# Two operand tiles behind the weights in SBUF, and four reorderings ahead of the first layer

## The chip, the core and the metric

The program runs on one core of one Trainium2 chip. The metric is the device time of one execution in microseconds (us), as a median of runs. A core has five engines that run side by side and wait for one another by semaphores: TensorE (PE, with weight loads listed as PEld), VectorE (DVE), ScalarE (ACT), GpSimd (POOL) and SyncE (SP, which here only issues DMA transfers). SBUF is the on-chip memory of 128 partitions; PSUM holds TensorE's results in eight banks.

## What is computed

```python
kv = np.einsum('bhsd,bhse->bhde', k, v)            # attention without softmax: 8 x 8 heads,
out = np.einsum('bhsd,bhde->bhse', q, kv)          # 576 tokens, 64 wide
out = out / sqrt(mean(out * out) + 1e-6) * g_norm
x = out.transpose(0, 2, 1, 3).reshape(4608, 512)

h = x @ w_in                                       # 512 -> 2048
g = np.maximum(h, 0.0) + alpha * np.minimum(h, 0.0)
x = g @ w_out                                      # 2048 -> 512

e = argmax(x @ w_gate + modality_bias[modality_id])  # one of 8 experts for each token
out[token] = gate * (relu(x @ w1[e]) @ w2[e])        # 512 -> 1024 -> 512
```

Every matrix product of the two dense stages is made of three: each fp32 operand is split in a high part, rounded to the fp32r type, and a low part, the remainder; high times high, high times low and low times high are summed in PSUM.

## The kernel before, in words

**Phase one** goes over the 4608 tokens in nine chunks of 512 (c = 0 to 8). In a chunk, 16 steps go over blocks of 128 of the 2048 hidden columns: `first` (L404) makes a block of h with 12 matmuls of 512 columns, and `second` (L431) adds the block before it to y with 12 more. In L404 the weights W are the stationary operand (128 columns, loaded ahead of each matmul) and x's parts, `xhi` and `xlo`, are the moving one (512 columns). In L431 the parts of g (tile g2, "g" in the rows) are stationary and W moves.

**Phase two** takes blocks of 128 tokens of one expert, 41 in all. Each has 24 matmuls of its first layer and 24 of its second, all recorded at L714. In the first layer `xhi` and `xlo` (which now hold the gathered rows' parts) are stationary and the expert's weights, again in W, move; in the second the parts of the hidden values (`hth`, `htl`) are stationary and W moves.

**SBUF.** The pool `one` lays its tiles out in the order in which the code allocates them, each start rounded up to 32 bytes. In the built program W begins at byte 4,224 of each partition and takes 131,072 bytes. Behind it come `ident`, `alpha_sb`, `less`, `g_sb`, four `yrow`, `tri`, `ones`, `wg_sb`, several small tables, two `kvbd` and `kx`, together 41,952 bytes, and only then `xhi` at byte 177,248 and `xlo` at 185,440 (8,192 bytes each). The tiles g2 and hth lie at 220,992 and 225,088, htl at 206,656, 210,752 or 214,848. So `xhi` and `xlo` start 32 bytes past a multiple of 64, as do the 128- and 512-column pieces that the matmuls read of them; W, g2, hth and htl and their pieces start on multiples of 64.

**PSUM.** Banks 0 to 3 belong to the pool `ps_y` (y, and ahead of phase one `kvp`, `ops` and `first`), banks 4 and 5 to `ps_h` (h), bank 6 to `a`, bank 7 is the tile `spare`. In phase two h takes banks 4 to 7.

**Ahead of the first layer**, the order on every engine is the order in which the code is written; there is no scheduler. For the first chunk, by function and line:

- `kv_pair(p)` (L284, L287): k'v of two heads on TensorE, copied to `kvbd` by VectorE (L289).
- `attend_pair(p)` (L293): the attention of two heads into four PSUM tiles `ops` (`a`, `spare` and two of `ps_y`).
- `square_half(t, h)` (L304, ScalarE) and `sum_half(t, h)` (L309, VectorE): squares and their sums for half the heads of token tile t, h = 0 for pairs 0 and 1, h = 1 for pairs 2 and 3.
- The first block of weights is rebuilt from its raw bits: `cut_a(0)` casts (L165, ScalarE), `low_bits(0)` (L174, VectorE), `high_bits(0)` joins both (L179, GpSimd), `cut_c(0)` writes W's high part (L190, ScalarE) and low part (L191, GpSimd).
- `rsqrt(0)`: `half` on GpSimd (L338), then VectorE's iteration from `u` (L339) to `root` (L345).
- `scale_first(h)` (L369): the scaled x, on VectorE for most tiles, on GpSimd for tile 2 and half of tile 3.
- `turn_first((0, 1))` and `turn_first((2, 3))` (L379): TensorE transposes x into four PSUM tiles, one for each block k of 128 columns.
- `take_x(0, k)`: xhi (L391, ScalarE) and xlo (L392, VectorE); then the loop begins with `first(0, 0)`, which takes its four xlo matmuls as late as it can.

A run of 36 transposes of the identity (`warm`, L885) keeps TensorE occupied while the scaling factors are made.

Of the kernel before, what the change touches and what calls it, by code (L numbers as in the profile page):

```python
# [8 lines left out]
F32 = mybir.dt.float32  # L9
F32R = mybir.dt.float32r  # L10
# [16 lines left out]
CT = 512  # L27
NT = CT // 128
# [22 lines left out]
def fused(ctx: ExitStack, tc, qT, kv, kv0, g2, wmoe, alpha, wgate, bias, modality, w12, out):  # L51
# [8 lines left out]
    one = ctx.enter_context(tc.tile_pool(name="one", bufs=1))  # L60
    two = ctx.enter_context(tc.tile_pool(name="two", bufs=2))
    dram = ctx.enter_context(tc.tile_pool(name="dram", bufs=1, space=DRAM))
    ps_y = ctx.enter_context(tc.tile_pool(name="ps_y", bufs=4, space=PSUM))
# [3 lines left out]
    spare = phase1.enter_context(tc.tile_pool(name="ps_s", bufs=1, space=PSUM)).tile([128, 512], F32, name="spare")  # L67
# [3 lines left out]
    xb = dram.tile([E * BUCKET + 1024, ROW], F32, name="xb")  # L71

    W = one.tile([128, 2 * SLOT], F32R, name="W")
    ident = one.tile([128, 128], F32, name="ident")
    alpha_sb = one.tile([128, NFB], F32, name="alpha_sb")
    less = one.tile([128, NFB], F32, name="less")
# [12 lines left out]
    kx = one.tile([128, 2560], F32, name="kx")  # L89
    xs = [kx[:, t * D:t * D + D] for t in range(NT)]  # L90
    xr = kx[:, 0:3 * D].rearrange("p (t c) -> p t c", c=D)
    xhi = one.tile([128, 4, CT], F32R, name="xhi")
    xlo = one.tile([128, 4, CT], F32R, name="xlo")
    junk = one.tile([128, D], F32, name="junk")
    tail = one.tile([128, NIT, 2], F32, name="tail")
    tab_pe = one.tile([1, 8], I32, name="tab_pe")
# [9 lines left out]
    def bank(n):  # L106
        return ps_h.tile([128, n], F32, tag="h", name="h")
# [28 lines left out]
    def w_at(fb, part):  # L136
        o = fb * 2048 + part * 512
        return W[:, o:o + 512]

# [20 lines left out]
    def cut_a(n):  # L160
        if n >= 2 * NFB:
            return

        a = yrow[(n + 1) % 3 if n else 0][:, 0:512]
        A.copy(a.bitcast(F16).rearrange("p (a b) -> p a b", b=2)[:, :, 1:2], raw_t[n].bitcast(BF16)[:, :, 2:3])  # L165
        cut_t[n] = a
# [111 lines left out]
    def kv_pair(p):  # L278

        t = kv_t.pop((0, p))  # L280
        kvp = ps_y.tile([128, 128], F32, tag="y", name="kvp") if p < 2 else bank(128)
        for k in range(4):
            o = k * 256
            PE.matmul(kvp, t[:, o:o + 128], t[:, o + 128:o + 256], start=(k == 0), stop=False)  # L284
        for o in (0, 64):
            r = slice(o, o + 64)
            PE.matmul(kvp[r, r], t[r, 1024:1088], t[r, 1088:1152], start=False, stop=True)  # L287
        for o in (0, 64):
            V.tensor_copy(kvbd[0][o:o + 64, p, o:o + 64], kvp[o:o + 64, o:o + 64])  # L289

    def attend_pair(p, ts=range(NT)):
        for t in ts:
            PE.matmul(ops[t][:, p, :], q_t[0][:, p, t * 128:(t + 1) * 128], kvbd[0][:, p, :], start=True, stop=True)  # L293
# [3 lines left out]
    def square_half(t, h):  # L297
        if t < 2:
            sq = (junk, yrow[3])[t][:, h * 256:h * 256 + 256]
        else:  # L300
            if not sq4:
                sq4.append(two.tile([128, CT], F32, tag="gg", name="sq", bufs=1))
            sq = sq4[0][:, (t - 2) * 256:(t - 1) * 256]
        A.activation(sq, ops[t][:, 2 * h:2 * h + 2, :].rearrange("p a b -> p (a b)"), AF.Square)  # L304
        sq_t[t, h] = sq

    def sum_half(t, h):
        o = t * 8 + h * 4
        V.tensor_reduce(ms_t[0][:, o:o + 4], sq_t.pop((t, h)).rearrange("p (a b) -> p a b", b=64), AX.X, ALU.add)  # L309
# [63 lines left out]
    first_x = []  # L373

    def turn_first(ks):
        pair = [ps_y.tile([128, CT], F32, tag="y", name="first") if k < 2 else spare if k == 2 else bank(CT) for k in ks]
        for t in range(NT):
            for k, ps in zip(ks, pair):
                PE.transpose(ps[:, t * 128:(t + 1) * 128], xs[t][:, k * 128:(k + 1) * 128], ident)  # L379
        return pair  # L380
# [255 lines left out]
    def load_expert(j, halves=(0, 1)):  # L636
# [4 lines left out]
        for half in halves:  # L641
# [3 lines left out]
            at = (j & 1) * SLOT + o  # L645
            d = SP.dma_start(W[:, at:at + SLOT // 2].bitcast(F32), wsp[ds(eid, 1), :, o:o + SLOT // 2].rearrange("a p c -> p (a c)"))
            tc.add_to_no_dep_group("experts", d.ins)
# [64 lines left out]
    def mm(i, ps, a, o, start, stop, late=False):  # L712
        w = (W if i < EARLY else regs[i][0])[:, o:o + 512]
        m = PE.matmul(ps, a, w, start=start, stop=stop)  # L714
        if i:
            tc.declare_no_dep(m.ins, group="experts", reason="sem_w says that the weights are in")
        if late:
            tc.declare_no_dep(m.ins, group=f"first half {i}", reason="of another bank")
# [3 lines left out]
    def layer1(i, between=None):  # L722
        if i >= EARLY:
# [5 lines left out]
            j, slot = PE.snap(j, min_val=0, max_val=7), PE.snap(slot, min_val=0, max_val=SLOT)  # L729
            regs[i] = W[:, ds(slot, SLOT)], j * 2 + 2  # L730
            PE.wait_ge(sem_w, j * 2 + 1)
# [129 lines left out]
    with tc.manual_schedule():  # L861
# [18 lines left out]
        def warm(n):  # L880
            if n == 0:
                return
            ps = bank(128)
            for _ in range(n):
                PE.transpose(ps, ident, ident)  # L885
# [12 lines left out]
        attend_pair(1)  # L898
        for t in range(NT):
            square_half(t, 0)  # L900
        kv_pair(3)
        for t in range(NT):
            sum_half(t, 0)
        attend_pair(2)
        attend_pair(3)
        for t in range(NT):
            square_half(t, 1)
        cut_a(0)
        warm(WARM[5])
        low_bits(0)  # L910
        high_bits(0)
# [16 lines left out]
        G.tensor_scalar(less, alpha_sb, -1.0, 1.0, ALU.mult, ALU.add)  # L928
        load_q(1)
        first_x.extend(turn_first((0, 1)) + turn_first((2, 3)))  # L930
        for k in range(4):
            take_x(0, k)
# [247 lines left out]
```

## Time and profile before

| | us |
|---|---|
| median of 3 runs | 1339.71 (1338.65 to 1340.37) |
| the profiled execution's own time | 1338.95 |
| its span, first to last instruction | 1337.3 |
| TensorE busy | 1326.1 (99%) |
| VectorE busy | 987.1 (74%) |
| GpSimd busy | 649.0 (49%) |
| ScalarE busy | 521.8 (39%) |

The profiled execution is 0.76 us under the median, and 1.65 us of it lie outside the span. A busy TensorE is not one at its peak: its matmuls overlap in the records (one lasts some 390 ns, while they start some 230 ns apart), so the distance between starts is read, from the timeline.

### The profile page before, as it was taken

The page shows a single profiled execution, that of the slowest core. Times are in us where ns is not written, and L with a number is a line of the kernel's source. Part 1 is how long each engine was busy: PE and PEld are TensorE (multiplying, and loading weights), DVE is VectorE, ACT ScalarE, POOL GpSimd, SP SyncE. Part 2 cuts the span into 40 slices and gives each one's busy share as a digit, 9 for nine tenths or more (in the row PEclk, how much of TensorE's full clock was granted, in tenths as well). Part 3 has the DMA queues.
Part 4 walks back from the last instruction along what each step waited for, and adds up shares of the span by engine and source line. Part 5 has one row for each costly group of instructions (what it writes and reads, how often), then busy time and mean ns, then how long its engine had stood idle before and what let it go on. Part 6 is the DMA issues. An engine that isn't in the chain of part 4 may idle for free.

```text
span 1337.3 us, 24668 instructions
## 1 busy us (share of the span) xinstructions
PE 1326.1 (99%) x8096; PEld 1074.1 (80%) x8096; DVE 987.1 (74%) x2052; ACT 521.8 (39%) x1093; POOL 649.0 (49%) x605
## 2 busy tenths in 40 slices
PE   9999999999999999999999999999999999999997
PEld 7878887888888878888888888788888888888886
DVE  5568977968959869869779779386766666666664
ACT  4665233233232332331332321154544444444443
POOL 4655556566465565565565652363333333333321
PEclk9999999999999999999999999999999999999999
DMA  9656456566376375475463530817411261737784
GB/s 339 226 176 217 162 201 228 176 229 227 126 257 213 107 265 189 143 272 170 161 234 113 190 116 0 306 41 258 177 48 48 84 260 49 283 104 297 295 332 175
DMA packets 81883, 250.56 MB, mean 187 GB/s; under 512 B 12829, under 2 KB 32029, under 8 KB 78560
## 3 DMA queue, kind: packets, MB, share of 16 engines
q1 hardware_dynamic: 70000, 220.82, 46.3%
q0 software_dynamic: 11760, 28.14, 6.5%
q8 instruction: 72, 1.18, 0.4%
q14 instruction: 51, 0.42, 0.1%
HBM read 158.69 MB, written 91.54 MB: 187 GB/s over the span
## 4 chain that ended last, share of the span: by engine, by line
PE 57%; issue 30%; POOL 5%; DVE 4%; DMA 2%; POOLq 2%; SPq 1%; ACT 0%; ACTq 0%; DVEq 0%
PE h L404 27%; PE y L431 26%; DVE junk L448 1%; PE a L240 1%; POOL kx L671 1%; POOL raw L227 1%; POOL g L417 1%; POOL out_dram L822 1%; DMA out_dram<-kvbd,tail 1%; POOLq L667 1%; PE a L265 1%; PE h L714 1%; POOLq L671 1%; PE spare L265 1%; DVE gg L410 0%
## 5 line engine op out<-in xcount | busy, mean ns | idle before, releaser
L431 PE MATMUL y<-W,g 128*128 128x512 f32 x1728 | 419.9, 392 | 0.9 <-ACT g L416 0.9
L404 PE MATMUL h<-xhi,W 128*128 128x512 f32 x1152 | 387.0, 398 | 0.0
L431 PEld LDWEIGHTS y<-W,g 128*128 128x128 f32 x1728 | 324.2, 188 | 74.1 <-ACT g L416 2.7
L417 POOL TENSOR_TENSOR g<-gg,g 128x512 fp32r<-128x512 f32 x144 | 216.8, 1506 | 335.4 <-ACT g L416 306.8
L448 DVE CUSTOM_DVE_ANT_0 junk<-yrow,wg_sb 128x512 f32<-128x512 f32 x256 | 273.9, 1070 | 6.4
L416 ACT CAST g<-gg 128x512 fp32r<-128x512 f32 x144 | 89.5, 621 | 441.2 <-DVE gg L411 387.2
L404 PEld LDWEIGHTS h<-xhi,W 128*128 128x128 f32 x1152 | 216.2, 188 | 52.0 <-issue 0.8
L404 PE MATMUL h<-xlo,W 128*128 128x512 f32 x576 | 225.9, 395 | 0.0
L714 PE MATMUL h<-W,xhi 128*128 (+1 forms) x656 | 206.4, 396 | 0.1
L714 PE MATMUL y<-W,hth 128*128 (+1 forms) x656 | 204.4, 393 | 0.0
L227 POOL TENSOR_TENSOR raw<-raw 128x512 f32<-128x512 f32 x128 | 193.6, 1517 | 14.9 <-ACT raw L223 14.7
L410 DVE TENSOR_SCALAR gg<-h,alpha_sb 128x512 f32<-128x512 f32 x128 | 95.7, 748 | 107.5 <-PE h L404 85.9
L822 POOL DMA_INDIRECT out_dram<-kvbd,tail x41 | 43.4, 1059 | 255.4 <-ACT kvbd L820 220.7
L714 PEld LDWEIGHTS h<-W,xhi 128*128 128x128 f32 x656 | 122.7, 187 | 30.2 <-issue 0.5
L714 PEld LDWEIGHTS y<-W,hth 128*128 128x128 f32 x656 | 123.1, 188 | 26.6
L768 DVE TENSOR_SCALAR hh<-h 32x256 f32<-32x256 f32 (+1 forms) x320 | 129.0, 403 | 7.4 <-PE h L714 2.4
L714 PE MATMUL h<-W,xlo 128*128 (+1 forms) x328 | 129.3, 394 | 0.0
L404 PEld LDWEIGHTS h<-xlo,W 128*128 128x128 f32 x576 | 108.2, 188 | 24.8 <-DVE xlo L392 0.3
L714 PE MATMUL y<-W,htl 128*128 (+1 forms) x328 | 127.6, 389 | 0.0
L768 ACT ACTIVATE hh<-h 32x256 f32<-32x256 f32 (+1 forms) x320 | 117.1, 366 | 23.3 <-PE h L714 17.7
L795 DVE TENSOR_TENSOR htl<-hh,hth 128x512 fp32r<-128x512 f32 x76 | 52.6, 693 | 97.5 <-ACT hth L788 97.4
L223 ACT CAST raw<-raw 128x512 fp32r<-128x512 f32 x128 | 78.5, 618 | 59.4 <-DMA raw<-in_w_dram 47.5
(226 smaller groups left out, 1262.3 us busy)
## 6 DMA issues: line engine op xcount, KB each, us to landing
wsp<-raw SPq DMA_DIRECT2D x128, 512.0 KB
W<-wsp SPq DMA_DIRECT2D x16, 4096.0 KB
raw<-in_w_dram SPq DMA_DIRECT2D x128, 256.0 KB
kx<-in_kv_dram SPq DMA_DIRECT2D x28, 512.0 KB
kx<-xb POOLq DMA_DIRECT2D x140, 64.0 KB
raw<-in_wmoe_dram SPq DMA_DIRECT2D x17, 511.8 KB
qT<-in_qT_dram SPq DMA_DIRECT2D x8, 1024.0 KB
wg_sb<-in_wmoe_dram SPq DMA_DIRECT2D x15, 511.8 KB
```

The costliest lines, as they stand in the source:

```text
L223: A.copy(sp_t[n][:, 0:512].bitcast(F32R), sp_t[n][:, 512:1024])
L227: G.tensor_tensor(lo, lo, hi, ALU.subtract)
L404: PE.matmul(ps, w_at(fb, part)[:, k * 128:(k + 1) * 128], x[:, k, :], start=(i == 0), stop=(i == 11))
L410: V.tensor_scalar(gg, ps, 0.0, alpha_sb[:, fb:fb + 1], ALU.min, ALU.mult)
L416: A.copy(ghi, gg)
L417: G.tensor_tensor(glo, gg, ghi.bitcast(F32), ALU.subtract)
L431: PE.matmul(y_t[c][t], a[:, t * 128:(t + 1) * 128], w, start=(fb == i == 0), stop=(fb == NFB - 1 and i == 2))
L448: V.tensor_tensor_reduce(junk, y, wg_sb[:, e, :], 1.0, 0.0, ALU.mult, ALU.add, lg_t[c][:, t, e:e + 1])
L714: m = PE.matmul(ps, a, w, start=start, stop=stop)
L768: m = V.tensor_scalar(to, of, 0.0, None, ALU.max) if mine else A.activation(to, of, AF.Relu)
L795: V.tensor_tensor(order(lo[:, n]), h[:, n].rearrange("p (a c j) -> p c a j", c=4, a=4), order(hi[:, n]).bitcast(F32), ALU.subtract)
L822: d = G.indirect_dma_start(out=out, out_offset=IndirectOffsetOnAxis(ap=tail[:, i, 1:2].bitcast(I32), axis=0), in_=y, in_offset=None, bound ...
```

## The change

`xhi` and `xlo` are allocated right behind W. In the built program they then start at 135,296 and 143,488, both multiples of 128; the tiles that stood between W and them move up by 16,384 bytes, and those behind them stay where they were. Nothing else of the loops changes: the same matmuls stand in the same order.

Ahead of the first layer, the sums of the first half come before `kv_pair(3)`, the weight's cast `cut_a(0)` before the second squares, and the turned block k = 2 goes to a tile of `ps_y` in the place of `spare`; `turn_first` takes the token tiles in the order 0, 2, 1, 3.

```diff
@@ tiles
     W = one.tile([128, 2 * SLOT], F32R, name="W")
+    xhi = one.tile([128, 4, CT], F32R, name="xhi")
+    xlo = one.tile([128, 4, CT], F32R, name="xlo")
     ident = one.tile([128, 128], F32, name="ident")
...
     xr = kx[:, 0:3 * D].rearrange("p (t c) -> p t c", c=D)
-    xhi = one.tile([128, 4, CT], F32R, name="xhi")
-    xlo = one.tile([128, 4, CT], F32R, name="xlo")
     junk = one.tile([128, D], F32, name="junk")
@@ turn_first
-        pair = [ps_y.tile([128, CT], F32, tag="y", name="first") if k < 2 else spare if k == 2 else bank(CT) for k in ks]
-        for t in range(NT):
+        pair = [ps_y.tile([128, CT], F32, tag="y", name="first") if k < 3 else bank(CT) for k in ks]
+        for t in (0, 2, 1, 3):
@@ ahead of the first layer
             square_half(t, 0)
-        kv_pair(3)
         for t in range(NT):
             sum_half(t, 0)
+        kv_pair(3)
         attend_pair(2)
         attend_pair(3)
+        cut_a(0)
         for t in range(NT):
             square_half(t, 1)
-        cut_a(0)
         warm(WARM[5])
```

On ScalarE, between the first squares and the copies of the attention's result, the program of before has these rows (a number behind a name tells buffers apart; yrow_83 is the weight's buffer):

```order
L304 ACTIVATE sq<-ops 128x256 x2
L304 ACTIVATE junk<-a 128x256
L304 ACTIVATE yrow_86<-spare 128x256
L304 ACTIVATE sq<-ops 128x256 x2
L165 CAST yrow_83<-raw 128x512
L915 COPY yrow_84<-ops 128x512
```

and the changed one these, where the weight's buffer is yrow_85:

```order
L304 ACTIVATE sq<-ops 128x256 x2
L165 CAST yrow_85<-raw 128x512
L304 ACTIVATE junk<-a 128x256
L304 ACTIVATE yrow_88<-spare 128x256
L304 ACTIVATE sq<-ops 128x256 x2
L915 COPY yrow_86<-ops 128x512
```

The cast of the first weight's raw bits has moved ahead of four squares.

On VectorE, from the copies of k'v to the end of the sums, before (kvbd_96 is the first of the two k'v tiles):

```order
L289 COPY kvbd_96<-h 64x64 x4
L309 TENSOR_REDUCE ms<-junk 128x4
L309 TENSOR_REDUCE ms<-yrow_86 128x4
L309 TENSOR_REDUCE ms<-sq 128x4 x2
L174 TENSOR_SCALAR wg_sb<-raw 128x512
```

and changed:

```order
L289 COPY kvbd_98<-h 64x64 x2
L309 TENSOR_REDUCE ms<-junk 128x4
L309 TENSOR_REDUCE ms<-yrow_88 128x4
L309 TENSOR_REDUCE ms<-sq 128x4 x2
L289 COPY kvbd_98<-h 64x64 x2
L174 TENSOR_SCALAR wg_sb<-raw 128x512
```

The four sums have moved ahead of the last two copies.

## Rows read from the trace of the kernel before

**Rows 1.** The page: busy time by engine, and TensorE's granted clock in tenths
```profile
PE 1326.1 (99%) x8096; PEld 1074.1 (80%) x8096; DVE 987.1 (74%) x2052; ACT 521.8 (39%) x1093; POOL 649.0 (49%) x605
...
PEclk9999999999999999999999999999999999999999
```

**Rows 2.** Timeline, TensorE, fifth chunk: start us, us, engine, line, operation, out<-in, count
```profile
399.55 4.74 PE L431 MATMUL y<-W,g 128*128 128x512 f32 x20
404.13 0.40 PE L404 MATMUL h<-xhi,W 128*128 128x512 f32 x1
...
406.93 1.08 PE L431 MATMUL y<-W,g 128*128 128x512 f32 x4
```

**Rows 3.** Timeline, TensorE, the two layers of expert blocks, same columns
```profile
1202.68 0.63 PE L714 MATMUL h<-W,xhi 128*128 x2
...
1208.05 0.39 PE L714 MATMUL h<-W,xlo 128*128 x1
1208.27 0.62 PE L714 MATMUL y<-W,hth 128*128 x2
...
1213.54 0.40 PE L714 MATMUL y<-W,htl 128*128 x1
```

**Rows 4.** The page's groups: line, engine, operation, out<-in, count | busy us, mean ns | idle
```profile
L404 PE MATMUL h<-xhi,W 128*128 128x512 f32 x1152 | 387.0, 398 | 0.0
...
L404 PE MATMUL h<-xlo,W 128*128 128x512 f32 x576 | 225.9, 395 | 0.0
L714 PE MATMUL h<-W,xhi 128*128 (+1 forms) x656 | 206.4, 396 | 0.1
...
L714 PE MATMUL h<-W,xlo 128*128 (+1 forms) x328 | 129.3, 394 | 0.0
```

**Rows 5.** Timeline, TensorE, attention of the first chunk, three PSUM tiles in turn
```profile
10.79 0.39 PE L293 MATMUL a<-kvbd,qT 128*128 128x128 f32 x2
...
11.01 0.39 PE L293 MATMUL spare<-kvbd,qT 128*128 128x128 f32 x2
...
11.23 0.61 PE L293 MATMUL ops<-kvbd,qT 128*128 128x128 f32 x4
```

**Rows 6.** Timeline, start to first layer; in brackets idle time and releaser
```profile
4.75 1.47 PEld L284 LDWEIGHTS kvp<-kx 128*128 128x128 f32 x8 [0.34 <-DMA kx<-in_kv_dram]
...
14.35 0.38 ACT L304 ACTIVATE junk<-a 128x256 f32<-128x256 f32 x1 [1.93 <-PE a L293]
...
15.42 0.80 ACT L165 CAST yrow<-raw 128x512 f16<-128x512 bf16 x1
...
15.84 0.73 DVE L309 TENSOR_REDUCE ms<-sq 128x4 f32<-128x256 f32 x2
...
16.35 1.28 POOL L179 TENSOR_TENSOR yrow<-yrow,wg_sb 128x512 int32<-128x512 int32 x1 [7.34 <-DVE ms L309]
...
17.97 0.19 DVE L339 TENSOR_TENSOR u<-h,half 128x32 f32<-128x32 f32 x1 [0.94 <-POOL half L338]
...
18.37 1.27 POOL L191 TENSOR_TENSOR W<-yrow,W 128x512 fp32r<-128x512 f32 x1 [0.43 <-ACT W L190]
...
20.31 1.21 PE L379 MATMUL first<-ident,kx 128*128 128x128 f32 x8 [1.40 <-DVE kx L369]
...
21.73 0.30 PE L379 MATMUL spare<-ident,kx 128*128 128x128 f32 x1 [0.21 <-DVE kx L369]
...
22.55 1.18 PE L404 MATMUL h<-xhi,W 128*128 128x512 f32 x4
...
24.15 0.74 DVE L392 SCALAR_TENSOR_TENSOR xlo<-h,g_sb,xhi 128x512 fp32r<-128x512 f32 x1
```

**Rows 7.** Windows: stretch, length, busy time by engine, clock, DMA share, GB/s
```profile
0.00:4.15 4.15, 2.58 (x12) 2.59 (x13) 0.97 (x2) 1.28 (x1) 3.19 (x25) 1.00 0.50 172
0.00:12.00 12.00, 10.38 (x73) 9.44 (x74) 2.30 (x8) 2.07 (x4) 3.75 (x26) 1.00 0.83 297
12.00:14.00 2.00, 2.00 (x20) 1.81 (x19) 0.91 (x4) 0.42 (x2) 0.00 (x0) 1.00 1.02 420
```

## The prediction, made before the changed kernel ran

> **What bounds the kernel now.** I read the page's shares first. [...] So nearly every microsecond is either a matmul's turn on TensorE or the start, and the question is how far apart matmuls start. That I read from starts in the timeline, not from the mean durations of some 390 ns, which overlap.
>
> In phase one, 20 matmuls of L431 go from 399.55 to 404.13, 4.58 us or 229.0 ns each, and then 12 of L404 from 404.13 to 406.93, 2.80 us or 233.3 ns each [rows 2]. In phase two the 24 of the first layer have 23 spacings from 1202.68 to 1208.05, 5.37 us or 233.5 ns each, and the 24 of the second 23 from 1208.27 to 1213.54, 5.27 us or 229.1 ns [rows 3]. All have 128 stationary and 512 moving columns of the same type, none waits, and yet there are two classes, 4.3 to 4.4 ns apart. The start has its own chain: TensorE waits 1.40 us for scaled x ahead of its first transposes, and VectorE 0.94 us for GpSimd ahead of that [rows 6].
>
> **The tiles' place.** What have the two slow classes in common? Not the shape, and not the role: xhi and xlo move in L404 and are stationary in phase two's first layer. W is in the quick classes as well. Two things are left: the slow ones alone read xhi and xlo, the only large operands here that start 32 bytes past a multiple of 64, and they write PSUM banks 4 to 7, the quick ones 0 to 3. Against the banks stands the first chunk's attention, which goes from bank 6 to bank 7 to two banks of the first four: groups start at 10.79, 11.01 and 11.23, two matmuls in 0.22 us in bank 6 as in bank 7, and the four of the last group take no longer each [rows 5] (these are 128-column matmuls, so they don't settle it). Distance from W doesn't fit either: the tiles at 206,656 and beyond are quick, those at 177,248 are slow, and W is as quick at its beginning as at its end, since L431 goes through all of it.
>
> For the start address speaks a size. [...] If both operands were read over one path, 640 columns in 229 ns would be 2.8 columns a nanosecond (an estimate from rows 2). An operand that begins in the middle of a 64-byte piece touches one piece more, 16 columns at most, 5.7 ns at that rate, and it does so once a matmul whether it has 128 columns or 512. The rows show 4.3 and 4.4 ns, once, in either role. The change puts both tiles on a multiple of 128, so I take the slow classes to become quick:
> - L404: 1152 + 576 = 1728 matmuls [rows 4] by 4.3 ns, 7.4 us.
> - Phase two's first layer: 656 + 328 = 984 [rows 4] by 4.4 ns, 4.3 us.
>
> Together 11.7 us. The bounds are nothing (the address is innocent) and, on the other side, one more such penalty in each (a rival below). No other engine stands in the way of a gain of 0.9%: VectorE stays under 75%. I leave up to 1 us for new short waits.
>
> **The start.** Today's chain is: second squares on ScalarE from 14.35, then the weight's cast from 15.42 for 0.80 us, then high_bits on GpSimd from 16.35 for 1.28 us, and only behind it `half`, for which VectorE waits until 17.97 [rows 6], though the sums that `half` is made of end at 15.84 + 0.73 = 16.57. With the cast earlier, high_bits is out of the way. How early can it be? ScalarE is idle for 1.93 us before 14.35, so from 12.42 on; the cast also needs the raw bits. Ahead of these and with them the queue moves four k'v pieces of 576 KB, two of q of 512 KB and 512 KB of bits, 3.93 MB by the code's shapes. By 12.00 it has moved 297 GB/s x 12.00 us = 3.56 MB, and the rest at 420 GB/s takes until 12.9 [rows 7]. From bytes moved to data usable is some 0.6 us or more: the first 0.59 MB were through before 4.15 (172 GB/s x 4.15 us = 0.71 MB [rows 7]), and TensorE started on them at 4.75 after waiting for that transfer [rows 6]. So the cast runs from about 13.6, bounds 13.4 and 14.2, to 14.5, and pushes the squares behind it by some 0.15 us. The second sums gain all the same, since the first four are done before the copies, in time in which VectorE waited: they end near 16.2. high_bits ends near 15.9, `half` can start at 16.3 and `u` at 16.7 in the place of 17.97: **1.25 us**. Bits at 14.2 would leave 0.7. At most 1.4 is to be had, TensorE's idle time: its 36 identity transposes end at 18.9.
>
> Behind `u` the rest moves along if GpSimd is free for its share of the scaling: L191 (1.27 us [rows 6]) starts once ScalarE has made W's high part, near 17.1, and ends near 18.45, when `root` is due at 18.5. That fits by a hair; a miss costs a tenth or two. The sums ahead of the copies of k'v delay these by under 0.1 us, hidden by the attention of pair 2, which stands ahead of the matmuls that need them. SP issues the same loads; one of them waits for the cast and gets free sooner, behind a queue that is full anyway.
>
> The third turned block: TensorE waits 0.21 us for VectorE before its transposes from 21.73 [rows 6], because `spare` is being read. With a bank of its own, and tiles 0 and 2 first, four of these eight transposes run ahead of that, and L404 can begin some 0.3 us sooner than 22.55. It ends in matmuls that need the last xlo, which VectorE finishes at 24.15 + 0.74 = 24.89; TensorE is some 0.25 us behind that today, so 0.25 is what counts; the bounds are nothing and 0.4.
>
> **Sum.** 1338.95 (the profiled execution) - 11.7 - 1.25 - 0.25 = 1325.75. The median is 0.76 above the profiled execution, so 1326.5. Own range: the start's 0.5 to 1.8, up to 1 us of new waits, and the classes' difference known to 0.5 ns over 2712 matmuls (1.4 us): 1324.5 to 1329.
>
> **Rivals.**
> 1. The address is innocent, the 4.3 ns belong to the PSUM bank or to something that I don't see; the start's 1.5 us are all there is: 1338.2, within 0.2% (2.7 us, about what a measurement of this kernel can tell from no change). For it: banks and addresses go together in rows 2 and 3. [...] Chance 0.14.
> 2. Only one role pays for its start address: if only the moving one, 1339.7 - 7.4 - 1.5 = 1330.8; if only the stationary one, 1339.7 - 4.3 - 1.5 = 1333.9. Against it: both classes show the same size. Chance 0.10.
> 3. Slower: in every quick class W sits on multiples of 128 and its partner (g2, hth, htl) 64 bytes past one. The change puts xhi, xlo and W all on multiples of 128. If the two reads of a matmul get into each other's way when they begin alike, each of the 2712 could lose what it now loses again: 1339.7 + 11.7 - 1.5 = 1349.9. It decides from 1.5 ns a matmul on: (1.5 + 2.7) us / 2712. No row has such a pair at this size. Chance 0.06.
>
> **How the numbers follow.** The forecast has 0.70, so 1326.5. Faster: forecast and second rival, 0.80; same: 0.14; slower: 0.06. The range from 1324.5 to 1335.0 takes in the forecast and the second rival, and leaves out the other two.
>
> **What would show it.** Right: in the changed trace, 12 matmuls of L404 in about 2.75 us and 23 spacings of phase two's first layer in about 5.27; the cast L165 near 13.6, `u` waiting hardly for GpSimd, first transposes near 19.05, L404 near 21.0. If L404 stays at 2.80 and the start has moved, the first rival holds; if one of the two layers alone has changed, the second; if they are at 2.85 and more, the third. If the cast starts after 14.2, the bits were late, and the start's term was too large.

## The result, and the profile after

The changed kernel takes 1325.16 us (1324.80 to 1325.68, 5 runs), the kernel before on the same chip 1339.55 us (1338.65 to 1340.37, 5 runs): a ratio of 0.9893, with a 95% interval from 0.988 to 0.9907. The prediction of 1326.5 is 1.3 us off. The sum came out right; two of its terms did not, and the reason given for the larger one was wrong, as the runs below show.

The page of the changed kernel, busy time by engine, granted clock, and two of TensorE's groups (count | busy us, mean ns | idle, and what ended it), answers [rows 1] and [rows 4]:

```profile
PE 1312.3 (99%) x8096; PEld 1074.2 (81%) x8096; DVE 984.8 (74%) x2052; ACT 522.0 (39%) x1093; POOL 650.5 (49%) x605
...
PEclk9999999999999999999999999999999999999999
...
L431 PE MATMUL y<-W,g 128*128 128x512 f32 x1728 | 420.1, 392 | 1.5 <-ACT g L416 1.5
...
L404 PE MATMUL h<-xhi,W 128*128 128x512 f32 x1152 | 381.3, 393 | 0.0
```

The granted clock (0.999 in both) and the counts are as before; TensorE is busy for 13.8 us less and the span is 13.5 us shorter (1337.3 to 1323.8 us). Nearly all of the change is in how far apart TensorE's matmuls start. The timeline of TensorE in the fifth chunk (start us, length us, engine, line, operation, out<-in, count), against [rows 2]:

```profile
395.36 4.74 PE L431 MATMUL y<-W,g 128*128 128x512 f32 x20
399.94 0.40 PE L404 MATMUL h<-xhi,W 128*128 128x512 f32 x1
...
402.68 1.08 PE L431 MATMUL y<-W,g 128*128 128x512 f32 x4
```

20 matmuls of L431 take 4.58 us, 229.0 ns each, to the hundredth as before. 12 of L404 take 2.74 us, 228.3 ns each, where they took 2.80. The same view in an expert block, against [rows 3]:

```profile
1190.20 0.62 PE L714 MATMUL h<-W,xhi 128*128 x2
...
1195.64 0.62 PE L714 MATMUL y<-W,hth 128*128 x2
...
1201.14 0.61 PE L714 MATMUL h<-W,xhi 128*128 x2
```

24 matmuls of the first layer now take 5.44 us (226.7 ns each), 24 of the second 5.50 (229.2 ns). In [rows 3] it is the other way round: the first layer's 24 have 5.59 us, from 1202.68 to 1208.27. So the slow class did not join the quick one, it went past it.

The start, timeline of all engines (in brackets idle time and what ended it), against [rows 6]:

```profile
14.99 0.77 ACT L165 CAST yrow<-raw 128x512 f16<-128x512 bf16 x1 [1.36 <-DMA raw<-in_wmoe_dram]
15.64 0.37 ACT L304 ACTIVATE junk<-a 128x256 f32<-128x256 f32 x1
...
15.91 1.28 POOL L179 TENSOR_TENSOR yrow<-yrow,wg_sb 128x512 int32<-128x512 int32 x1 [5.82 <-ACT yrow L165]
...
18.01 0.19 DVE L339 TENSOR_TENSOR u<-h,half 128x32 f32<-128x32 f32 x1
...
20.34 1.38 PE L379 MATMUL first<-ident,kx 128*128 128x128 f32 x9 [0.21 <-DVE kx L369]
...
22.24 1.18 PE L404 MATMUL h<-xhi,W 128*128 128x512 f32 x4
```

The cast does stand ahead of the second squares, but it waits 1.36 us for the raw bits, and the squares wait behind it, from 14.35 before to 15.64. `u` no longer waits for GpSimd and is still at 18.01 (17.97 before). L404 begins 0.31 us sooner.

**The account.** I take starts of TensorE's matmuls from both traces, and a mean spacing over all those under 245 ns, so that waits do not enter. From the first L404 to phase two the time fell from 849.71 to 841.85 us, in phase two from 457.71 to 452.32; with 0.31 at the start, less 0.09 that the stretch behind TensorE's last start grew, that is the span's 13.5 us. The spacings alone give more: L404 232.9 to 227.7 ns, times 1728, is 9.0 us; the first layer 233.3 to 226.8 ns, times 984, is 6.4. About 2 us of these 15.4 were lost again: some 1.6 in spacings over 245 ns, which hold waits, and 0.5 because L431 and the second layer, which were not moved, had spacings 0.25 and 0.1 ns longer than before. TensorE's waits in the changed kernel (engine, line, waited for: us in total, times, longest):

```profile
PE y L431 <- ACT g L416: 1.5, 4, 0.6
PE kvp L284 <- DMA kx<-in_kv_dram: 0.5, 1, 0.5
...
PE first L379 <- DVE kx L369: 0.2, 1, 0.2
```

The wait for ScalarE's g was 0.9 us before; the one for kx, a load that came late in this execution, is new; the last one was 1.40 us in [rows 6].

### The profile page after: what moved, and what is told of

The parts are those of the page before. It is cut to its first block, busy times and chain, and to the rows that moved or that the text cites. A ratio compares the mean times of both kernels' runs of the same rounds, so it can differ in the third digit from the quotient of the medians.

```text
span 1323.8 us, 24667 instructions
## 1 busy us (share of the span) xinstructions
PE 1312.3 (99%) x8096; PEld 1074.2 (81%) x8096; DVE 984.8 (74%) x2052; ACT 522.0 (39%) x1093; POOL 650.5 (49%) x605
## 4 chain that ended last, share of the span: by engine, by line
PE 46%; issue 32%; POOL 8%; DVE 5%; DMA 5%; POOLq 2%; SPq 1%; ACT 1%; ACTq 0%; DVEq 0%
PE h L404 22%; PE y L431 21%; POOL raw L227 3%; POOL g L417 2%; DVE junk L448 2%; POOL kx L671 1%; DMA raw<-in_w_dram 1%; PE a L240 1%; POOL out_dram L822 1%; DMA out_dram<-kvbd,tail 1%; POOLq L667 1%; DMA raw<-in_wmoe_dram 1%; DMA xb<-yrow 1%; DVE gg L410 1%; DVE gg L411 1%
## 5 line engine op out<-in xcount | busy, mean ns | idle before, releaser
L431 PE MATMUL y<-W,g 128*128 128x512 f32 x1728 | 420.1, 392 | 1.5 <-ACT g L416 1.5
L431 PEld LDWEIGHTS y<-W,g 128*128 128x128 f32 x1728 | 324.0, 188 | 73.8 <-ACT g L416 3.4
L404 PE MATMUL h<-xhi,W 128*128 128x512 f32 x1152 | 381.3, 393 | 0.0
L404 PEld LDWEIGHTS h<-xhi,W 128*128 128x128 f32 x1152 | 216.0, 188 | 47.7 <-issue 0.8
L404 PE MATMUL h<-xlo,W 128*128 128x512 f32 x576 | 223.1, 390 | 0.0
L714 PE MATMUL h<-W,xhi 128*128 (+1 forms) x656 | 202.3, 390 | 0.3 <-PE y L714 0.3
L404 PEld LDWEIGHTS h<-xlo,W 128*128 128x128 f32 x576 | 108.2, 188 | 22.0 <-DVE xlo L392 0.3
L768 ACT ACTIVATE hh<-h 32x256 f32<-32x256 f32 (+1 forms) x320 | 117.4, 367 | 18.5 <-PE h L714 14.2
```

What stands on the lines that cost most here:

```text
L404: PE.matmul(ps, w_at(fb, part)[:, k * 128:(k + 1) * 128], x[:, k, :], start=(i == 0), stop=(i == 11))
L431: PE.matmul(y_t[c][t], a[:, t * 128:(t + 1) * 128], w, start=(fb == i == 0), stop=(fb == NFB - 1 and i == 2))
L768: m = V.tensor_scalar(to, of, 0.0, None, ALU.max) if mine else A.activation(to, of, AF.Relu)
```

## Experiments

The theory on record was that `xhi` and `xlo` pay for their own start in the middle of a 64-byte piece. The rivals were that the place is innocent (the PSUM banks, or the reordering, bring the gain), and that it is not a tile's own start that counts but how it stands to W's.

### The change in its two halves

Only the tiles' move, in the old order:

```diff
     W = one.tile([128, 2 * SLOT], F32R, name="W")
+    xhi = one.tile([128, 4, CT], F32R, name="xhi")
+    xlo = one.tile([128, 4, CT], F32R, name="xlo")
...
-    xhi = one.tile([128, 4, CT], F32R, name="xhi")
-    xlo = one.tile([128, 4, CT], F32R, name="xlo")
     junk = one.tile([128, D], F32, name="junk")
```

> Only the tiles' move (xhi at 135,296, xlo at 143,488), the order ahead of the first layer as before. If the start address or the nearness to W makes the gain, matmul spacings of L404 and of the expert blocks' first layer are those of the changed kernel (about 227.5 and 226.7 ns, from 233) and the time is 1325.5 to 1326.7, short of the changed kernel's 1325.2 by what the reorderings are worth (0.3 us by its profile, 1.5 by the prediction). If the reorderings make a part of the gain that I do not see, it stays above 1328.

Measured: 1330.01 us against 1341.64, ratio 0.9921 (0.9907 to 0.9934), 11.6 us less. The spacings are those of the changed kernel, 227.7 and 226.9 ns for the moved tiles' two classes, 229.0 for the others. The PSUM banks are the same as before, and the moved tiles' spacings fell from 232.9 and 233.3 ns all the same, so the banks are not what costs. The time is above the 1328 that the expectation named for a further effect of the order, but the kernel before is also 2.1 us slower on this chip than on the first. The 11.6 us here and the 1.4 of the next run make 13.0; the changed kernel gains 14.2 where it runs again below, and the intervals are wide enough for that.

Only the reorderings, with the tiles where they were:

```diff
+        for t in range(NT):
+            sum_half(t, 0)
         kv_pair(3)
-        for t in range(NT):
-            sum_half(t, 0)
...
+        cut_a(0)
         for t in range(NT):
             square_half(t, 1)
-        cut_a(0)
```

and `turn_first` as in the change.

> Only the reorderings, xhi and xlo in their old place. By the prediction 1.5 us less than before, 1338.1; by the two profiles, in which the first layer begins 0.3 us sooner, 1339.2. The spacings stay at 233 ns in the slow classes. In the profile: when the first weight's raw bits are usable (13.65 us before, 14.9 changed) and where the cast and u then stand tells whether late bits or the order itself ate the gain.

Measured: 1340.26 us, ratio 0.999 (0.998 to 1.0), 1.4 us less and just at the limit of what can be told. All four spacings are as before (232.9, 228.7, 233.3, 228.9 ns). So the two halves are separate: the place changes the spacings, the order does not.

### Which property of the place

Old place, but moved up by 32 bytes to a multiple of 128:

```diff
+    gap0 = one.tile([128, 8], F32, name="gap0")
     xhi = one.tile([128, 4, CT], F32R, name="xhi")
     xlo = one.tile([128, 4, CT], F32R, name="xlo")
+    gap1 = one.tile([128, 24], F32, name="gap1")
```

> The kernel before with a gap of 32 bytes ahead of xhi (and 96 behind xlo, so that all later tiles keep their place within 128 bytes): xhi at 177,280, a multiple of 128, still 41,984 bytes behind W. If the start address decides, both slow classes fall to about 227 ns and the time to 1325 to 1327. If nearness to W decides, nothing moves: 1339.5.

Measured: 1340.94 us, ratio 0.9993 (0.9984 to 1.0003), no change. The expectation missed that the gaps, 128 bytes in all, also push g2, hth and htl from byte 64 of a 256-byte piece to byte 192. The timeline of an expert block shows what followed:

```profile
1193.76 0.62 PE L716 MATMUL h<-W,xhi 128*128 x2
...
1199.23 0.63 PE L716 MATMUL y<-W,hth 128*128 x2
...
1204.83 0.62 PE L716 MATMUL h<-W,xhi 128*128 x2
```

The first layer's 24 fell to 5.47 us (5.59 in [rows 3]), and the second layer's rose from 5.50 to 5.60. The same in phase one: L404 229.4 ns, L431 232.9. A start on a multiple of 64 did not keep hth and g2 quick: byte 64 and byte 192 are both multiples of 64, and at the one g2 and hth had 228.7 and 228.9 ns, at the other 232.9 and 233.1. The 64-byte story was in trouble here.

New place, moved up by 32 bytes; the gaps stand behind W:

```diff
     W = one.tile([128, 2 * SLOT], F32R, name="W")
+    gap0 = one.tile([128, 8], F32, name="gap0")
     xhi = one.tile([128, 4, CT], F32R, name="xhi")
     xlo = one.tile([128, 4, CT], F32R, name="xlo")
+    gap1 = one.tile([128, 24], F32, name="gap1")
```

> The changed kernel with a gap of 32 bytes between W and xhi: xhi at 135,328, right behind W but 32 bytes past a multiple of 128. If the start address decides, the slow classes are back at 233 ns and the time at 1338 to 1340. If nearness decides, 1325.

Measured: 1349.51 us, ratio 1.0061 (1.0046 to 1.0077): slower than before, since xhi and xlo are 32 bytes off W again, now on the other side, and here too g2 and hth went to byte 192. Both layers of a block are slow, 5.59 and 5.60 us:

```profile
1190.11 0.63 PE L716 MATMUL h<-W,xhi 128*128 x2
...
1195.70 0.63 PE L716 MATMUL y<-W,hth 128*128 x2
...
1201.30 0.63 PE L716 MATMUL h<-W,xhi 128*128 x2
```

Nearness to W did not help: the first layer's 24 take 5.59 us right behind W, as at the old place. The new idea was then that the offset between the two operands counts. If it does, g2 and hth can be made to gain as well, by 64 bytes ahead of them that bring them to byte 128, where W starts:

```diff
     star = one.tile([1, E], F32, name="star")
+    gap0 = one.tile([128, 16], F32, name="gap0")
```

> The changed kernel with a gap of 64 bytes behind the last small tile of the pool, so that g2, hth and htl move from byte 64 to byte 128 of a 256-byte piece, where W, xhi and xlo start. The theory after the first four runs: a matmul is quickest (227 ns) when its two operands start at the same byte of a 256-byte piece, 229 when the partner starts 64 bytes lower than W, 233 at the other offsets seen. By it L431 and the second layer fall from 229 to about 227.5 and 226.8, 1728 x 1.5 + 984 x 2.2 = 4.8 us, and the time is some 5 us under the changed kernel on the same chip. If only xhi and xlo count, nothing changes.

and beside it, on the same chip, the changed kernel once more:

> The changed kernel as it is, for comparison on the same chip, and a second look at its start: if the first layer begins 7.33 us after the first weight's raw bits are usable (as in the three profiles with the new order so far: 14.91 and 22.24, 14.23 and 21.56, 13.80 and 21.13), the order works and late bits are what took its gain; if not, another wait does.

Measured: 1324.11 us (1321.69 to 1327.67), ratio 0.9861 (0.9844 to 0.9877), against 1327.82 us (1326.86 to 1329.06), ratio 0.9892 (0.9875 to 0.9908), for the changed kernel. Both layers of a block now take 5.44 us:

```profile
1192.35 0.62 PE L715 MATMUL h<-W,xhi 128*128 x2
...
1197.79 0.62 PE L715 MATMUL y<-W,hth 128*128 x2
...
1203.23 0.62 PE L715 MATMUL h<-W,xhi 128*128 x2
```

The spacings of L431 and of the second layer fell to 226.9 and 226.8 ns. By its median this version beats both kernels; the two intervals overlap at 0.9875 to 0.9877, so the spacings show the gain more surely than the time does. Against the changed kernel it gained 3.7 us of the 5.6 that the spacings promise ((228.9 - 226.9) ns x 1728 and (229.0 - 226.8) ns x 984). Its profiled execution, the longest of its four, shows where more can go; TensorE's waits:

```profile
PE y L432 <- ACT g L417: 3.1, 4, 1.0
...
PE h L715 <- ACT xhi L702: 1.4, 1, 1.4
PE y L432 <- ACT yrow L443: 1.4, 1, 1.4
PE y L715 <- SPq L655: 1.3, 1, 1.3
```

Such waits may grow as TensorE gets to the same places sooner; that is not shown, since they also differ between executions: the changed kernel's second profile has 2.0, 1.8 and 1.0 us of such waits, its first 1.5.

**The offset alone.** Two kernels move everything from W on by 64 and by 32 bytes, so that every tile's own start changes and no offset does:

```diff
+    gap0 = one.tile([128, 16], F32, name="gap0")
     W = one.tile([128, 2 * SLOT], F32R, name="W")
```

and the same with 8 in the place of 16.

> The changed kernel with a gap of 64 bytes ahead of W: W, xhi and xlo all start at byte 192 of a 256-byte piece, g2, hth and htl at 128. If the offset between the two operands decides, nothing changes: L404 and the first layer stay near 227, L431 and the second layer near 229, 1325 us. If each tile's own start decides, and byte 128 is the good one, W, xhi and xlo are now all off it, and L404 and the first layer rise to 233.

> The changed kernel with a gap of 32 bytes ahead of W: W, xhi, xlo, g2, hth and htl all start 32 bytes past a multiple of 64, with the offsets between them as in the changed kernel. If offsets alone decide, L404 and the first layer stay near 227, L431 and the second layer near 229. If a start in the middle of a 64-byte piece costs something by itself, as the prediction had it, all four go to 233 or more, and the time to 1340 or above.

Measured (one run each, on two chips): 1328.29 us, beside 1327.82 for the changed kernel on the same chip, and 1328.27 us, where the kernel before took 1341.34. With 32 bytes every operand starts 32 past a multiple of 64, what the prediction held to be the trouble, and a block still shows 5.44 and 5.49 us:

```profile
1193.68 0.62 PE L715 MATMUL h<-W,xhi 128*128 x2
...
1199.12 0.62 PE L715 MATMUL y<-W,hth 128*128 x2
...
1204.61 0.62 PE L715 MATMUL h<-W,xhi 128*128 x2
```

That refutes the prediction's mechanism: with both operands in the middle of a 64-byte piece the two layers take 5.44 and 5.49 us, and in the changed kernel, where neither is, 5.44 and 5.50. Two more kernels set x 64 bytes below and above W's offset; the first by allocating `alpha_sb` and `bsel` (1,216 bytes) between W and `xhi`, the second by a gap of 64 bytes there, which also moves g2 and hth to byte 128:

```diff
     W = one.tile([128, 2 * SLOT], F32R, name="W")
+    alpha_sb = one.tile([128, NFB], F32, name="alpha_sb")
+    bsel = one.tile([128, NTOK // 128, E], F32, name="bsel")
     xhi = one.tile([128, 4, CT], F32R, name="xhi")
```

```diff
     W = one.tile([128, 2 * SLOT], F32R, name="W")
+    gap0 = one.tile([128, 16], F32, name="gap0")
     xhi = one.tile([128, 4, CT], F32R, name="xhi")
```

> The changed kernel with alpha_sb and bsel (1,216 bytes) between W and xhi: xhi and xlo start at byte 64 of a 256-byte piece, 64 lower than W, where g2, hth and htl are. If the offset decides, L404 and the first layer come to 229 like L431 and the second layer, some 4 us over the changed kernel (1728 x 1.3 + 984 x 2.2 ns). If nearness to W or a multiple of 128 is what xhi needs, 233, some 15 us over.

> The changed kernel with a gap of 64 bytes between W and xhi: xhi and xlo start 64 bytes higher than W in a 256-byte piece (192), g2, hth and htl at the same byte as W (128). What the eight runs so far add up to: the spacing goes by the byte at which the stationary operand starts less that of the moving one, within 256: 0 gives 227 ns, 64 lower 229, 32 either way and 64 higher 233. By it L404, where x moves and W is stationary, comes to 229, the first layer of phase two, where x is stationary, to 233, L431 and the second layer to 227: the mirror image of the run before. If x's own start decides and not the roles, L404 and the first layer come out alike.

Measured (one run each): 1339.5 and 1337.0 us. Expert blocks, x 64 bytes below W:

```profile
1193.41 0.62 PE L714 MATMUL h<-W,xhi 128*128 x2
...
1198.91 0.62 PE L714 MATMUL y<-W,hth 128*128 x2
...
1204.40 0.62 PE L714 MATMUL h<-W,xhi 128*128 x2
```

and x above:

```profile
1190.09 0.63 PE L715 MATMUL h<-W,xhi 128*128 x2
...
1195.69 0.62 PE L715 MATMUL y<-W,hth 128*128 x2
...
1201.16 0.63 PE L715 MATMUL h<-W,xhi 128*128 x2
```

The first layer takes 5.50 us with x below W and 5.60 with x above, so the sign matters; I had expected of x below that both its classes take 229 ns, and L404, where x is the operand that moves, took 233.1. With x above it is the mirror image. All of it in one table: the offset is the stationary operand's start less the moving one's, within 256 bytes, and behind it stands the mean spacing in ns (of those under 245), worked out from the traces.

| kernel | L404 | first layer | L431 | second layer |
|---|---|---|---|---|
| before | +32: 232.9 | -32: 233.3 | -64: 228.7 | -64: 228.9 |
| changed | 0: 227.7 | 0: 226.8 | -64: 228.9 | -64: 229.0 |
| old place, up 32 | 0: 229.4 | 0: 227.9 | +64: 232.9 | +64: 233.1 |
| new place, up 32 | -32: 232.9 | +32: 233.1 | +64: 233.1 | +64: 233.4 |
| all alike | 0: 227.4 | 0: 226.8 | 0: 226.9 | 0: 226.8 |
| all up 64 | 0: 227.7 | 0: 226.8 | -64: 229.0 | -64: 228.9 |
| all up 32 | 0: 227.7 | 0: 226.8 | -64: 228.9 | -64: 228.9 |
| x 64 below | +64: 233.1 | -64: 228.9 | -64: 231.2 | -64: 228.9 |
| x 64 above | -64: 230.0 | +64: 233.2 | 0: 230.6 | 0: 227.9 |

Offset 0 goes with some 227 ns, -64 with 229, +32, -32 and +64 with 233; in the two columns of the expert blocks this holds within 1.1 ns. A period of 128 is excluded, since +64 and -64 differ (233.1 and 228.9 ns in the second layer); 256 is enough for these runs, since in the kernel with all alike g2 stands 256 bytes from W within 512, x stands at 0, and both are quick (226.9 and 227.4 ns).

In phase one four entries are 1 to 4 ns longer than their offset says (229.4, 231.2, 230.0 and 230.6). The single spacings in the traces show where that comes from: a run of matmuls of one class need not begin at its offset's spacing. With the old place up 32, L404's first seven spacings are, to 1 ns, 229, 231, 231, 236, 228, 233 and 231 ns and the rest 226 or 227, in 98 of its 101 runs of 12 that are recorded whole and without a wait; the same seven stand at the head of the 24 in the two expert-block entries of 227.9. With x above, L404 takes five matmuls in most of its runs to settle at 229, and L431 reaches 227 only with the twelfth in 108 of 124. With x below, 27 of L431's 124 runs stay at 231 to 236 throughout. So in these runs the class that ran before counted as well for the first matmuls of a run, and runs of 12 paid more for it than runs of 24 (229.4 ns against 227.9 with the old place up 32). What in the chip makes the offset count, and a run settle, is open. Offsets of 96 and 128 were not tried.

### The start

The changed kernel with the cast back behind the squares:

```diff
         attend_pair(3)
-        cut_a(0)
         for t in range(NT):
             square_half(t, 1)
+        cut_a(0)
```

> The changed kernel with cut_a(0) back behind the second squares; sums, third turn and layout as changed. If the cast's place makes the start's gain, from the first of the second squares to the first matmul of L404 it is some 7.9 us (8.2 in the order of before, less 0.3 for the third turn), and not 6.6 as with the changed order; the second squares begin when the attention is done and do not wait for the bits.

Measured: 1327.79 us (one run), and in the timeline of the start:

```profile
14.80 0.38 ACT L304 ACTIVATE junk<-a 128x256 f32<-128x256 f32 x1 [1.93 <-PE a L293]
...
15.87 0.80 ACT L165 CAST yrow<-raw 128x512 f16<-128x512 bf16 x1
...
18.43 0.19 DVE L339 TENSOR_TENSOR u<-h,half 128x32 f32<-128x32 f32 x1 [1.35 <-POOL half L338]
...
22.67 0.71 PE L404 MATMUL h<-xhi,W 128*128 128x512 f32 x2
```

From the second squares to L404 it is 7.87 us here, 22.67 - 14.80. Before it is 8.20 (22.55 - 14.35), and so it is, within 0.01, in the two other kernels with the old order. In the nine profiles with the new order it is 6.59 to 6.63, so the cast's place is worth 1.25 us and the rest of the reordering 0.33. Whether this shows went with when the raw bits were in. In the changed kernel's first profile they were usable at 14.91 us, and in its second they came earlier:

```profile
13.73 0.77 ACT L165 CAST yrow<-raw 128x512 f16<-128x512 bf16 x1 [0.82 <-DMA raw<-in_wmoe_dram]
...
14.84 0.38 ACT L304 ACTIVATE junk<-a 128x256 f32<-128x256 f32 x1 [0.34 <-PE a L293]
...
17.22 0.19 DVE L339 TENSOR_TENSOR u<-h,half 128x32 f32<-128x32 f32 x1
...
21.46 0.71 PE L404 MATMUL h<-xhi,W 128*128 128x512 f32 x2
```

Here the cast is done before TensorE has finished the attention that the squares read, and L404 begins at 21.46, 1.09 us sooner than before. Over thirteen profiles the bits were usable between 13.47 and 14.91 us. L404 begins between 20.97 and 22.24 in the nine profiles with the new order, 21.43 in the mean, and between 22.55 and 23.03 in the three with the old one, 22.71 in the mean: 1.3 us sooner, and the changed kernel's first profile is the latest of the nine.

## Why the prediction was right, and where it was not

**What bounds the kernel** held: a gain of 1% came almost wholly out of TensorE's spacings, and no other engine's total limited it (VectorE, the next, was busy for 984.8 of 1323.8 us).

**The tiles' place** was the right suspect. Of its arguments, that neither the shape nor the bank makes the class was borne out by the move alone, with the same matmuls in the same banks (232.9 to 227.7 ns in L404). The role did not matter at 32 bytes, where both signs are slow (232.9 to 233.3 ns), but it did at 64: with x below W the same tiles cost 233.1 ns as the moving operand and 228.9 as the stationary one. Two steps failed. One is the mechanism: "an operand that begins in the middle of a 64-byte piece touches one piece more". With everything moved by 32 bytes L404 and the first layer took 227.7 and 226.8 ns, as without. That the operands are read over one path, in pieces of 64 bytes, was an assumption of the prediction, which no run shows, and the size fitted the 4.3 ns by accident; that `xhi` and `xlo` alone start 32 past a multiple of 64 was true, but so was that they alone stood 32 bytes off W, and the prediction's list of what the slow classes share did not ask that: "Distance from W doesn't fit either" took the distance as a length, where it is its remainder within 256 bytes that the spacings went with, from 227 ns at 0 to 233 at 32. It came near in its third rival, that the two reads get in each other's way when they "begin alike", with the sign reversed: alike was the quickest (226.8 ns in the first layer), and it is the kernel with offsets of 32 and 64 throughout that takes about the time of that rival (1349.51 us). The other failed step is the size: "I take the slow classes to become quick". The quick classes were themselves at an offset of -64 (229 ns) and not at 0 (227), so L404 and the first layer gained 5.2 and 6.5 ns, not 4.3 and 4.4: 15.4 us in the place of 11.7.

**Rivals.** The first (the place is innocent, 1338.2) fell with the move alone, 0.9921. The second (one role pays) fell with the spacings, since both roles gained (5.2 and 6.5 ns). The third is the one above.

**The start** was sized rightly and timed wrongly. The order is worth 1.58 us from the squares on, where the prediction had 1.25 and 0.25. The step that failed is "the cast runs from about 13.6, bounds 13.4 and 14.2": it ran from 14.99 in the profile after, and the prediction's own sign for that, a cast after 14.2, was met. The bits' arrival was worked out from one execution's rows; between executions it varies by 1.4 us, as much as the term itself. What shows in the median is the reordering's 1.4 us by itself, with an interval from 0 to 2.7.

**New waits** were given up to 1 us and left out of the sum; some 1.6 us came, and 0.5 of longer spacings in the classes that did not move. So 3.7 us too little for the place stand against some 1.2 too much for the start (0.31 for 1.5) and these 2 us, and these nearly cancel: 13.5 us less in the profiled span, where the sum had 13.2. That the time came within 1.3 us is luck; what was right is that the place of the two tiles costs most of it.

## What to carry to other kernels

Where the same matmuls run at spacings a few nanoseconds apart, compare the start bytes of the two SBUF operands with each other, not each with a round number, and try giving every pair the same byte within 256: here it cost a gap of 64 bytes, and all four spacings came to 226.8 to 227.4 ns. These runs have one shape and one type only. Before a property that the costly instructions share is taken for the cause, list those that relate one operand to the other. A step that waits for a load should not be put ahead of work that has its data, unless the load's latest arrival, over several executions, is earlier than that work: here the cast waited 1.36 us for its bits with four squares behind it.

## What the runs showed of the hardware

- The spacing of 128x128 by 512 matmuls of type fp32r depended on the offset between the starts of stationary and moving operand: 24 took 5.44 us at 0 (5.47 behind a class at +64), 5.49 to 5.50 at -64, and 5.59 to 5.60 at +32, -32, +64. Their common start did not matter (227.7 ns in L404 and 226.8 in the first layer with shifts of 32 and 64 bytes as without).
- At offset 0 the single spacings are 226 or 227 ns; at -64 they go 226, 229, 232 over and over (both in the changed kernel's trace). Behind a class at another offset it took up to eleven matmuls to get there, and at -64, behind +64, 27 of 124 runs of 12 did not.
- With gaps of 32 and 96 bytes around xhi and xlo in their new place the kernel was 0.6% slower than before, 1349.51 us against 1341.64: all four pairs of operands then stood at -32, +32 or +64, with 232.9 to 233.4 ns.
- The first load of raw weight bits became usable between 13.47 and 14.91 us, in kernels that issue the same loads ahead of it.
